# One wait fewer on ScalarE: the exponential of a score tile's first half and VectorE's copy of the second

## The chip, the cores and the metric

The kernel runs on one core of one Trainium2 chip. The metric is device time in microseconds (us) of one launch, the median of several runs. Five engines work side by side, each through its own list of instructions in order: TensorE (PE in the profile, with its weight loads shown apart as PEld), VectorE (DVE), ScalarE (ACT), GpSimd (POOL) and SyncE (SP, which starts the DMA transfers here). An instruction that needs another engine's result waits on a semaphore, and everything behind it on its own engine waits too. Matmul results land in PSUM, which has eight banks; a bank holds 512 float32 values for each of 128 partitions.

## What is computed

The reference mixes an attention branch and a feed-forward branch over the same input `x` (2048 rows of 512):

```python
g = _sigmoid((x * gate_w).sum(-1, keepdims=True))
q = (x @ wq) in 32 heads of 16;  k = x @ wk;  v = x @ wv      # one k and v for all heads
p = _softmax(einsum("bhqd,bkd->bhqk", q, k) * 16 ** -0.5)
a = (p @ v, heads side by side) @ wo
b = (_silu(x @ w_gate) * (x @ w_up)) @ w_down                 # 1792 hidden features
return g * a + (1 - g) * b
```

Everything is float32. The 32 x 2048 x 2048 exponentials of the attention are the bulk of ScalarE's work, and the feed-forward matmuls are run in three terms each (high and low parts), which is the bulk of TensorE's.

## The kernel before

A first stage (to about 48 us) transposes `x` and makes keys, values and the first queries. A second one (to about 141 us) runs the first 16 loop turns of the attention in a simple pattern. The main stage, from 141 us to 1480 us, is made of blocks, and the change is in it. A tail (83 us) multiplies by `wo` and stores the output.

**A block.** The attention is cut into units `u`: one head and 128 keys against all 2048 queries. A block issues the scores of four units, works on their exponentials, and ends with `mix` (L662 to L671), the product of exponentials and values, for four units whose scores are a little older. Each unit has two score tiles, so a block has eight, numbered 0 to 7 here. A score tile `ps` (named `pss` in the profile) is 128 x 1024: two matmuls at L651, one for each half, and each half fills a PSUM bank of its own. Only two score tiles exist (`ps_s` has two buffers), so the matmuls of tile i+2 wait until tile i has been read.

**TensorE's order in a block** is written out in `STEPS = "SSFFFFSFFSFFSFFFSFFFSFFS"`. S is a score tile. F is a step of the feed-forward work: two matmuls side by side in the two halves of the array (L174). So between tile 2 and tile 3 there are two F, and so on. After the last S comes `mix` (L670).

**Who reads a score tile.** `KINDS = "HHHAHHAA"` says it. An A tile (3, 6, 7) is read by ScalarE alone, in one exponential over 1024 columns. An H tile (0, 1, 2, 4, 5) is shared: VectorE copies its second half out of PSUM into the tile `pt` in SBUF (L656), and ScalarE takes the exponential of its first half straight from PSUM (L660, `pt<-pss 128x512`). The second half's exponential is done later, in place in SBUF (L660, `pt<-pt 128x512`).

**ScalarE's order** is the list `EXPS = ("0d", "1d", "0s", "2d", "3d", "4d", "1s", "5d", "6d", "7d", "2s", "4s", "5s")`: `d` is the exponential out of PSUM, `s` the one in place of the copied half. At the end of some blocks a tanh of the feed-forward work follows (L268 or L272).

**VectorE's order** follows the program text: the copies stand behind their score tiles, the evacuations of finished feed-forward tiles in between, and at the end of a block up to 3.6 us (`BUDGET`) of put-off work: the silu product that needs the tanh (L276), splits into high and low parts, reciprocals of the softmax sums (L679).

The framework below the kernel puts in all the semaphore waits. It keeps any two instructions that touch the same tile `ps` in order, so before the change the exponential of an H tile's first half waits for the copy of its second half, though the two touch neither the same PSUM bank nor the same columns of `pt`.

Of the kernel before, what the change touches and what calls it, by code (L numbers as in the profile page):

```python
# [12 lines left out]
AF = mybir.ActivationFunctionType  # L13
# [8 lines left out]
H = 32  # L22
# [4 lines left out]
CH = 512  # L27
# [7 lines left out]
SCALE = DH ** -0.5  # L35
# [26 lines left out]
def tile_gated_mix(ctx, tc, x, wq, wk, wv, wo, w_gate, w_up, w_down, gate_w, out):  # L62
    nc = tc.nc
# [59 lines left out]
    def run(queue, n):  # L123
        for _ in range(min(n, len(queue))):
            queue.pop(0)()
# [502 lines left out]
    with tc.tile_pool(name="bpool", bufs=2) as bp:  # L628
# [11 lines left out]
        def new_pt(u):  # L640
            late = u > PTB * (BEGIN * 2 // PTB) and (u - 2 * BEGIN) % (2 * PTB) >= PTB
            PT[u] = (PAIR[1] if late else bp).tile([P, S], F32, name="pt", bufs=PTB)

        def score(u, j, half=False):
            h, kt = divmod(u, NT)
            if j == 0:
                new_pt(u)
            ps = ps_s.tile([P, 2 * CH], F32, name="pss")
            for b in range(2):
                rows = slice(b * RT, (b + 1) * RT)  # L650
                nc.tensor.matmul(ps[:, b * CH:(b + 1) * CH], ks[rows, kt * P:(kt + 1) * P], QS[h][rows, j, :],  # L651
                                 start=True, stop=True)
            halves.clock += 1
            pt = PT[u][:, j * 2 * CH:(j + 1) * 2 * CH]
            if half:
                nc.vector.tensor_copy(pt[:, CH:], ps[:, CH:])  # L656
            return pt, ps

        def exps(pt, ps, w=slice(None)):
            nc.scalar.activation(pt[:, w], ps[:, w], AF.Exp, scale=SCALE)  # L660

        def mix(u):  # L662
            h, kt = divmod(u, NT)
            pt = PT.pop(u)
            if kt == 0:
                run(COPY, 1)
                PO[:] = [ps_o.tile([P, CH], F32, name="po")]
            po = PO[0]
            for c in range(NCH):
                nc.tensor.matmul(po[c * 2 * DH:(c + 1) * 2 * DH, :], vaug[:, kt, :], pt[:, c * CH:(c + 1) * CH],  # L670
                                 start=(kt == 0), stop=(kt == NT - 1))  # L671
            if kt == NT - 1:

                osb = hp.tile([P, CH], F32, name="osb")
                rsb = hp.tile([P, CH], F32, name="rsb", bufs=1)

                def invert(i):
                    w = slice(i * P, (i + 1) * P)
                    nc.vector.reciprocal(rsb[:, w], rsb[:, w])  # L679

                def store():
                    nc.vector.tensor_tensor(osb, osb, rsb, ALU.mult)
                    for c in range(NCH):
                        nc.sync.dma_start(o_d[h * DH:(h + 1) * DH, c * CH:(c + 1) * CH],
                                          osb[c * 2 * DH:c * 2 * DH + DH, :])

                COPY.append(lambda: nc.vector.tensor_copy(osb, po))
                LATER.extend([(0.6, lambda: nc.vector.stream_shuffle(rsb, osb, [DH] * 2 * DH))] +
                             [(1.0, lambda i=i: invert(i)) for i in range(TC)] + [(0.7, store)])
# [5 lines left out]
        def feed(k, more=True):  # L695
            for _ in range(k):
                if JOBS and more or halves.busy():
                    halves.step(more)

        def block(k, first, last, steps, kinds, order):  # L700
            more = k < NB - STOP
            tiles = [(u, j) for u in range(first, last) for j in range(2)]
            order = list(order)
            made = []

            def emit():
                while order and int(order[0][0]) < len(made):
                    i, how = int(order[0][0]), order.pop(0)[1]
                    pt, ps = made[i]
                    if how == "s":  # L710
                        exps(pt, pt, slice(CH, None))
                    else:
                        exps(pt, ps, slice(0, CH) if kinds[i] == "H" else slice(None))

            for i, what in enumerate(steps):
                if what == "F":
                    feed(1, more)
                elif len(made) < len(tiles):
                    made.append(score(*tiles[len(made)], kinds[len(made)] == "H"))
                    emit()  # L720
                if len(made) > 1:
                    run(COPY, 1)
            due = [e for e in order if int(e[0]) < 2 * (BLOCK * (k + 1) - first)]
            for e in due:
                order.remove(e)
            rest, order[:] = order[:], due
            emit()
            run(ACTS, len(ACTS))
            order[:] = rest
            emit()  # L730
            assert not order and len(made) == len(tiles)
            left = BUDGET
            for queue in (LATER[:1], DEFER, LATER):
                while queue and queue[0][0] <= left:
                    cost, f = queue.pop(0)
                    left -= cost
                    f()
                if queue is not DEFER and queue is not LATER and left < BUDGET:
                    LATER.pop(0)
            for u in range(BLOCK * k, BLOCK * (k + 1)):  # L740
                mix(u)
            halves.clock += 2 * LONG
# [7 lines left out]
        with tc.manual_schedule():  # L750
            for j in range(2):
                exps(*score(0, j))
            for n in range(BEGIN):
                quota = RATE
                u = 2 * n
                if n == 0:
                    feed(FIRST)
                exps(*score(u + 1, 0))
                if n == 0:
                    feed(quota - FIRST)  # L760
                exps(*score(u + 1, 1))
                feed(FIRST)
                exps(*score(u + 2, 0))
                feed(quota - FIRST)
                exps(*score(u + 2, 1))
                settle()
                mix(u)
                mix(u + 1)
                halves.clock += LONG
                run(COPY, 1)  # L770
                if LATER:
                    LATER.pop(0)[1]()
                if n == NT // 2 + 1:
                    load_head(2)
# [59 lines left out]
    with tc.If(rv != 0):  # L834
        with tc.tile_pool(name="gpool", bufs=2) as gp:
            with tc.For_i(0, H, 1) as h:
# [3 lines left out]
                for qt in range(NT):  # L840
# [3 lines left out]
                    for half in range(2):  # L844
                        ps = ps_s.tile([P, 2 * CH], F32, name="pss")
# [8 lines left out]
                    for half in range(2):  # L854
                        nc.scalar.activation(pr[:, half * 2 * CH:(half + 1) * 2 * CH], halves[half], AF.Exp,
                                             scale=SCALE, bias=mx[:, 2:3])
                    po = ps_o.tile([P, CH], F32, name="po")
                    for b in range(NT // TC):
                        pt = ps_f.tile([P, CH], F32, name="pf")
# [48 lines left out]
```

## Time and profile before

| what | value |
|---|---|
| median of 3 runs | 1564.16 us (1563.3 to 1565.58) |
| the profiled execution: its own time | 1565.49 us |
| its span, first to last instruction | 1563.7 us |
| TensorE busy | 1433.5 us (92%) |
| TensorE weight loads | 761.6 us (49%) |
| ScalarE busy | 1089.2 us (70%) |
| VectorE busy | 862.9 us (55%) |
| GpSimd busy | 389.0 us (25%) |
| mean granted TensorE clock | 0.989 |

Busy time of TensorE counts matmuls that overlap, and a matmul that was held up shows a longer duration, so 92% doesn't mean that only 8% could be gained. In a row of the timeline stand the start, the duration, the engine, the source line, the operation, the tiles written and read, the shape and the count; the bracket behind it gives idle time of the engine just before and the instruction that ended it. In the list of waits stand the waiting group, the releasing group, the total in us, how often, and the longest. A group's row gives its busy time and the mean duration in ns.

### The profile page before, as it was taken

The numbers are of one execution on the slowest core, as the hardware profiler recorded it, in microseconds if no ns is written. First come the engines' busy times: TensorE is split into PE (matmuls) and PEld (weight loads), VectorE is DVE, ScalarE is ACT, GpSimd is POOL, SyncE is SP. The second block draws the span as 40 slices with busy tenths as digits, with TensorE's granted clock in tenths as the row PEclk, the third lists the DMA queues.
The fourth block names the chain that finished last, engine by engine and source line by source line (L and its number), as shares of the span: only waits on it lengthen the run. The fifth ranks groups of instructions, "written<-read, shape, count | busy, mean of one in ns | idle before, by whom it ended". The sixth has DMA issues, their size and how long they took to land. (4 is left out here: it accounts for less than half of the span.)

```text
span 1563.7 us, 26910 instructions
## 1 busy us (share of the span) xinstructions
PE 1433.5 (92%) x10755; PEld 761.6 (49%) x10755; DVE 862.9 (55%) x1458; ACT 1089.2 (70%) x1699; POOL 389.0 (25%) x408
## 2 busy tenths in 40 slices
PE   9999999998989988999898988989999889899998
PEld 7654444444444444444444444444444444454476
DVE  5464555565555565556456566456556556465442
ACT  4677777777777767777777777777777777777700
POOL 5041220420220410230130331141131230143153
PEclk9999999999999999999999999999999999999999
DMA  7554211211131310211131221120221120221044
GB/s 244 179 167 119 63 38 31 68 32 41 50 103 31 105 41 24 56 48 36 53 112 31 72 51 45 31 82 25 58 58 30 62 64 25 58 65 51 12 151 143
DMA packets 101493, 107.79 MB, mean 69 GB/s; under 512 B 9969, under 2 KB 69617, under 8 KB 99697
## 3 DMA queue, kind: packets, MB, share of 16 engines
q1 hardware_dynamic: 99632, 105.81, 23.4%
q8 instruction: 86, 1.41, 0.4%
q10 hardware_dynamic: 1728, 0.20, 0.1%
q14 instruction: 47, 0.38, 0.1%
HBM read 76.09 MB, written 29.36 MB: 67 GB/s over the span
## 5 line engine op out<-in xcount | busy, mean ns | idle before, releaser
L660 ACT ACTIVATE pt<-pss 128x512 f32<-128x512 f32 (+1 forms) x1024 | 746.1, 779 | 371.6 <-DVE pt L656 337.5
L656 DVE COPY pt<-pss 128x512 f32<-128x512 f32 x590 | 395.3, 687 | 363.1 <-PE pss L651 356.5
L651 PE MATMUL pss<-qs,ks 64*128 64x512 f32 x2048 | 454.9, 457 | 117.6 <-ACT pt L660 113.4
L670 PE MATMUL po<-pt,vaug 128*32 128x512 f32 x4096 | 467.7, 596 | 0.0
L651 PEld LDWEIGHTS pss<-qs,ks 64*128 64x128 f32 x2048 | 185.5, 186 | 442.1 <-ACT pt L660 329.4
L660 ACT ACTIVATE pt<-pt 128x512 f32<-128x512 f32 x590 | 345.8, 637 | 0.0
L670 PEld LDWEIGHTS po<-pt,vaug 128*32 128x32 f32 x4096 | 119.5, 110 | 258.1 <-issue 257.8
L105 POOL CAST wuh<-wraw 128x512 fp32r<-128x512 f32 x56 | 34.5, 617 | 553.6 <-PE pf L174 431.1
L174 PE MATMUL pf<-xh,wuh 64*128 64x512 f32 (+1 forms) x440 | 168.1, 398 | 0.0
L174 PE MATMUL pf<-xh,wgh 64*128 64x512 f32 (+1 forms) x444 | 167.0, 395 | 0.0
L174 PE MATMUL pf<-xh,wgl 64*128 64x512 f32 (+1 forms) x444 | 166.6, 395 | 0.0
L174 PE MATMUL pf<-xl,wgh 64*128 64x512 f32 (+1 forms) x444 | 166.3, 395 | 0.0
L174 PE MATMUL pf<-xh,wul 64*128 64x512 f32 (+1 forms) x440 | 165.6, 396 | 0.0
L174 PE MATMUL pf<-xl,wuh 64*128 64x512 f32 (+1 forms) x440 | 164.7, 397 | 0.0
L174 PE MATMUL pf<-wdl,hh 64*128 64x512 f32 (+1 forms) x427 | 160.3, 397 | 2.5 <-POOL wdl L106 2.5
L174 PE MATMUL pf<-wdh,hl 64*128 64x512 f32 (+1 forms) x427 | 160.0, 397 | 0.0
L174 PE MATMUL pf<-wdh,hh 64*128 64x512 f32 (+1 forms) x427 | 158.5, 397 | 0.4 <-POOL wdh L105 0.4
L105 POOL CAST wgh<-wraw 128x512 fp32r<-128x512 f32 x56 | 35.2, 629 | 413.7 <-PE pf L174 330.7
L679 DVE RECIPROCAL rsb<-rsb 128x128 f32<-128x128 f32 x128 | 115.9, 931 | 2.8 <-issue 1.2
L276 DVE SCALAR_TENSOR_TENSOR ht<-ht,hs 128x512 f32<-128x512 f32 x48 | 34.1, 711 | 133.2 <-ACT ht L268 133.2
L174 PEld LDWEIGHTS pf<-xl,wuh 64*128 64x128 f32 (+1 forms) x440 | 83.4, 190 | 7.7
L174 PEld LDWEIGHTS pf<-xh,wuh 64*128 64x128 f32 (+1 forms) x440 | 83.5, 190 | 7.0
(157 smaller groups left out, 1637.0 us busy)
## 6 DMA issues: line engine op xcount, KB each, us to landing
wraw<-in_B_w_gate_dram SPq DMA_DIRECT2D x56, 256.0 KB
wraw<-in_B_w_up_dram SPq DMA_DIRECT2D x56, 256.0 KB
wraw<-in_B_w_down_dram SPq DMA_DIRECT2D x56, 256.0 KB
qs<-q_d SPq DMA_DIRECT2D x62, 192.0 KB
q_d<-hl SPq DMA_DIRECT2D x18, 256.0 KB
q_d<-hh SPq DMA_DIRECT2D x18, 256.0 KB
o_d<-osb SPq DMA_DIRECT2D x128, 32.0 KB
a_d<-acc SPq DMA_DIRECT2D x4, 1024.0 KB
```

The source lines that it names most:

```text
L105: eng_hi.tensor_copy(hi, src)
L174: ins = nc.tensor.matmul(self.ps, a, b, start=(i == 0 and not half), stop=(last and half != 0))
L276: nc.vector.scalar_tensor_tensor(t[0], t[0], 1.0, g, op0=ALU.add, op1=ALU.mult)
L651: nc.tensor.matmul(ps[:, b * CH:(b + 1) * CH], ks[rows, kt * P:(kt + 1) * P], QS[h][rows, j, :], start=True, stop=True)
L656: nc.vector.tensor_copy(pt[:, CH:], ps[:, CH:])
L660: nc.scalar.activation(pt[:, w], ps[:, w], AF.Exp, scale=SCALE)
L670: nc.tensor.matmul(po[c * 2 * DH:(c + 1) * 2 * DH, :], vaug[:, kt, :], pt[:, c * CH:(c + 1) * CH], start=(kt == 0), stop=(kt == NT - 1))
L679: nc.vector.reciprocal(rsb[:, w], rsb[:, w])
```

## The change

The function `score` now returns VectorE's copy instruction along with the tile. The function `exps` tells the framework that the exponential of an H tile's first half doesn't depend on that copy. Which instruction stands where on each engine stays the same; what changes is what some of them wait for.

```diff
-            if half:
-                nc.vector.tensor_copy(pt[:, CH:], ps[:, CH:])
-            return pt, ps
-
-        def exps(pt, ps, w=slice(None)):
-            nc.scalar.activation(pt[:, w], ps[:, w], AF.Exp, scale=SCALE)
+            other = nc.vector.tensor_copy(pt[:, CH:], ps[:, CH:]) if half else None
+            return pt, ps, other
+
+        def exps(pt, ps, other=None, w=slice(None)):
+            ins = nc.scalar.activation(pt[:, w], ps[:, w], AF.Exp, scale=SCALE)
+            if other is not None:
+                tc.declare_no_dep(getattr(ins, "ins", ins), getattr(other, "ins", other), reason="another bank")
...
-                    pt, ps = made[i]
+                    pt, ps, other = made[i]
                     if how == "s":
-                        exps(pt, pt, slice(CH, None))
+                        exps(pt, pt, w=slice(CH, None))
                     else:
-                        exps(pt, ps, slice(0, CH) if kinds[i] == "H" else slice(None))
+                        exps(pt, ps, other, slice(0, CH) if kinds[i] == "H" else slice(None))
```

ScalarE, one block of before, its thirteen exponentials in the order of `EXPS`; a name like DVE_49 is the semaphore that counts VectorE's instructions, PE_49 and Activation_49 those of TensorE and ScalarE:

```order
L660 ACTIVATE pt<-pss 128x512 [waits DVE_49,Activation_49]
L660 ACTIVATE pt<-pss 128x512 [waits DVE_49]
L660 ACTIVATE pt<-pt 128x512
L660 ACTIVATE pt<-pss 128x512 [waits DVE_49]
L660 ACTIVATE pt<-pss 128x1024 [waits PE_49]
L660 ACTIVATE pt<-pss 128x512 [waits DVE_49]
L660 ACTIVATE pt<-pt 128x512
L660 ACTIVATE pt<-pss 128x512 [waits DVE_49]
L660 ACTIVATE pt<-pss 128x1024 [waits PE_49,Activation_49]
L660 ACTIVATE pt<-pss 128x1024 [waits PE_49]
L660 ACTIVATE pt<-pt 128x512 x3
```

The same block of the changed kernel (L659 is the same statement, which stands one line higher there):

```order
L659 ACTIVATE pt<-pss 128x512 [waits PE_49,Activation_49]
L659 ACTIVATE pt<-pss 128x512 [waits PE_49]
L659 ACTIVATE pt<-pt 128x512 [waits DVE_49]
L659 ACTIVATE pt<-pss 128x512 [waits PE_49]
L659 ACTIVATE pt<-pss 128x1024 [waits PE_49]
L659 ACTIVATE pt<-pss 128x512 [waits PE_49]
L659 ACTIVATE pt<-pt 128x512 [waits DVE_49]
L659 ACTIVATE pt<-pss 128x512 [waits PE_49]
L659 ACTIVATE pt<-pss 128x1024 [waits PE_49,Activation_49]
L659 ACTIVATE pt<-pss 128x1024 [waits PE_49]
L659 ACTIVATE pt<-pt 128x512 [waits DVE_49] x3
```

Nothing moved. The five exponentials of first halves wait for the score matmul instead of the copy, and the five in place now name the copy, which they had behind them already before.

TensorE, score tiles 2 and 3 of a block, before:

```order
L651 MATMUL pss<-qs,ks 128x512 [waits Activation_49]
L651 MATMUL pss<-qs,ks 128x512
L174 MATMUL pf<-wdh,hl 128x512
L174 MATMUL pf<-wdh,hh 128x512 x2
L174 MATMUL pf<-wdl,hh 128x512
L651 MATMUL pss<-qs,ks 128x512 [waits Activation_49]
```

And in the changed kernel:

```order
L651 MATMUL pss<-qs,ks 128x512 [waits DVE_49,Activation_49]
L651 MATMUL pss<-qs,ks 128x512
L174 MATMUL pf<-wdh,hl 128x512
L174 MATMUL pf<-wdh,hh 128x512 x2
L174 MATMUL pf<-wdl,hh 128x512
L651 MATMUL pss<-qs,ks 128x512 [waits DVE_49,Activation_49]
```

A score tile that reuses the place of an H tile now waits for both of its readers by name. An instruction carries one wait; a second one becomes an instruction of its own ahead of it, EVENT_SEMAPHORE in the profile. So TensorE's list grows by 590 of these, five for each of 118 blocks, and ScalarE's by 28.

## The prediction

> **What bounds the kernel now.** I began with the page's busy times and the list of waits.
>
> ```profile
> PE 1433.5 (92%) x10755; PEld 761.6 (49%) x10755; DVE 862.9 (55%) x1458; ACT 1089.2 (70%) x1699; POOL 389.0 (25%) x408
> ```
>
> ```profile
> ACT pt L660 <- DVE pt L656: 337.5, 344, 4.0
> PEld pss L651 <- ACT pt L660: 329.4, 573, 2.3
> PE pss L651 <- ACT pt L660: 113.4, 240, 1.9
> ```
>
> No engine is full apart from TensorE's 92%, which counts overlapped and held-up matmuls. The three waits form one chain: ScalarE stands 337.5 us behind VectorE's copies, and TensorE's score tiles stand behind ScalarE. The edit cuts the first link. What that is worth depends on when the copy ends compared with the exponential, so I read one ordinary block in the timeline, first TensorE:
>
> ```profile
> 730.84 0.73 PE L651 MATMUL pss<-qs,ks 64*128 64x512 f32 x4
> 731.41 0.39 PE L174 MATMUL pf<-wdl,hh 64*128 64x512 f32 x1
> ...
> 732.10 0.39 PE L174 MATMUL pf<-wdl,hh 64*128 64x512 f32 x1
> ...
> 732.82 0.50 PE L651 MATMUL pss<-qs,ks 64*128 64x512 f32 x2 [0.32 <-ACT pt L660]
> ...
> 733.62 0.40 PE L651 MATMUL pss<-qs,ks 64*128 64x512 f32 x2
> ...
> 734.73 0.50 PE L651 MATMUL pss<-qs,ks 64*128 64x512 f32 x2 [0.25 <-ACT pt L660]
> ...
> 735.77 0.41 PE L651 MATMUL pss<-qs,ks 64*128 64x512 f32 x2
> ...
> 736.73 0.51 PE L651 MATMUL pss<-qs,ks 64*128 64x512 f32 x2
> ...
> 737.73 0.50 PE L651 MATMUL pss<-qs,ks 64*128 64x512 f32 x2
> 738.16 3.64 PE L670 MATMUL po<-pt,vaug 128*32 128x512 f32 x32
> 741.73 0.73 PE L651 MATMUL pss<-qs,ks 64*128 64x512 f32 x4
> ```
>
> Tiles 0 and 1 start at 730.84 and about 731.18, four F steps follow, and the block ends at 741.73: 10.89 us. An undisturbed step takes 0.23 (731.41 to 732.10 is three steps) to 0.24 (735.77 to 736.73 is four); I use 0.235. Against that, tile 2 should start at 731.41 + 4 x 0.235 = 732.35 and starts at 732.82; tile 4 should start three steps after tile 3, at 734.32, and starts at 734.73; tile 7 comes at 737.73 instead of 737.43. A tile that was held also makes the next step 0.1 longer (732.82 to 733.62 is 0.80, not 0.70). Then ScalarE and VectorE in the same stretch:
>
> ```profile
> 732.17 1.13 ACT L660 ACTIVATE pt<-pss 128x512 f32<-128x512 f32 x2 [2.01 <-DVE pt L656]
> 733.20 0.62 ACT L660 ACTIVATE pt<-pt 128x512 f32<-128x512 f32 x1
> 734.09 1.51 ACT L660 ACTIVATE pt<-pss 128x512 f32<-128x512 f32 x2 [0.27 <-DVE sign L394]
> 736.08 0.60 ACT L660 ACTIVATE pt<-pss 128x512 f32<-128x512 f32 x1 [0.48 <-DVE pt L656]
> 736.57 0.62 ACT L660 ACTIVATE pt<-pt 128x512 f32<-128x512 f32 x1
> 737.09 2.42 ACT L660 ACTIVATE pt<-pss 128x512 f32<-128x512 f32 x3
> 739.38 1.69 ACT L660 ACTIVATE pt<-pt 128x512 f32<-128x512 f32 x3
> ```
>
> ```profile
> 731.38 1.29 DVE L656 COPY pt<-pss 128x512 f32<-128x512 f32 x2 [0.74 <-PE pss L651]
> 733.36 0.69 DVE L656 COPY pt<-pss 128x512 f32<-128x512 f32 x1 [0.69 <-PE pss L651]
> ...
> 735.35 0.69 DVE L656 COPY pt<-pss 128x512 f32<-128x512 f32 x1 [1.30 <-PE pss L651]
> 736.22 0.69 DVE L656 COPY pt<-pss 128x512 f32<-128x512 f32 x1 [0.18 <-PE pss L651]
> ```
>
> Each held tile is the same relay. Tile 0's matmul starts at 730.84, the copy runs 731.38 to 732.07, ScalarE starts only at 732.17 (idle for 2.01 before) and ends at 732.77, and TensorE starts tile 2 at 732.82. Copy and exponential stand one behind the other, and the ring of two score tiles passes both on to TensorE.
>
> **The change, an ordinary block replayed by hand.** The wait for the copy goes; the exponential may start when the matmul is done, as the copy does: 0.54 after a tile's start behind `mix` (731.38 - 730.84), 0.44 else (a matmul of 0.40 and a gap of about 0.04). ScalarE starts its 512-column pieces 0.52 apart (736.57 to 737.09) and the 1024-column ones 0.9 apart (737.09 to 739.38 is one short and two long).
>
> - Tile 0: exponential 731.38 to 731.98, copy to 732.07. Tile 1: exponential 731.9 to 732.5, copy to 732.67 (731.38 + 1.29). The in-place piece 0s runs 732.4 to 733.0, its copy long done.
> - Tile 2 needs tile 0 free at 732.07 and is due at 732.35: no wait. Tile 3 is due at 733.05 and needs 732.67.
> - Tile 2's copy runs 732.8 to 733.5, its exponential 732.9 to 733.5, behind 0s. Tile 4 is due at 733.76: no wait.
> - Tile 3 (ScalarE alone) 733.5 to 734.5; tile 5 is due at 734.70. Tile 4's exponential ends at 735.0, its copy at 734.9; tile 6 is due at 735.64. Tile 5's exponential, behind 1s, ends at 736.0 and its copy at 735.8; tile 7 is due at 736.35.
> - Tile 7 to `mix` takes 0.43 as now, `mix` to the next block 3.57 as now: `mix` at 736.78, the next block at 740.35.
>
> So this block takes 9.51 us, not 10.89: 1.38 less. What is late next there is nothing on ScalarE (the smallest margin is about 0.2, ahead of tile 5) but TensorE's own list. ScalarE's 13 pieces take 10 x 0.52 + 3 x 0.9 = 7.9 of the 9.5 us. The new waits of the five in-place pieces cost nothing while the copy is done first, as here; if VectorE were late, everything behind 0s on ScalarE would wait with it, tile 2's exponential first.
>
> How many blocks there are, and how long the mean one is:
>
> ```profile
> L656 DVE COPY pt<-pss x590: 625/691/695, 141.5 to 1472.2; 128x512 f32<-128x512 f32 x197
> ```
>
> 590 copies at five a block are 118 blocks. From the first block's first copy to the last block's last one are 1330.7 us; less the 4.84 between those two in a block (731.38 to 736.22), 1325.9 / 117 = 11.33 us for the mean block, 0.44 over the ordinary one. One of those that are longer:
>
> ```profile
> 706.59 0.69 DVE L276 SCALAR_TENSOR_TENSOR ht<-ht,hs 128x512 f32<-128x512 f32 x1 [3.82 <-ACT ht L268]
> ...
> 707.97 0.39 PE L174 MATMUL pf<-wdl,hh 64*128 64x512 f32 x1
> ...
> 708.17 0.69 DVE L682 TENSOR_TENSOR osb<-osb,rsb 128x512 f32<-128x512 f32 x1
> ...
> 708.78 1.28 DVE L656 COPY pt<-pss 128x512 f32<-128x512 f32 x2
> ...
> 709.56 1.14 ACT L660 ACTIVATE pt<-pss 128x512 f32<-128x512 f32 x2 [3.01 <-DVE pt L656]
> ...
> 710.21 0.56 PE L651 MATMUL pss<-qs,ks 64*128 64x512 f32 x2 [1.85 <-ACT pt L660]
> ```
>
> Here VectorE sat behind the tanh, then worked off what was put off, and copied tile 0 only at 708.78. Tile 2 was due at 707.97 + 0.235 = 708.2 and came at 710.21, 2.0 late. After the edit it still needs the copy, done at 709.45, so it comes at 709.5, 1.3 late: it saves 0.7 at this tile where the ordinary block saves 0.47. The excess of long blocks therefore does not grow; I carry the 0.44 over whole.
>
> The sum: 9.51 + 0.44 = 9.95 us. I add 0.05 for VectorE, which has less room once blocks are shorter: 10.0, 1.33 less than 11.33. Times 118: 157 us. The profiled execution took 1565.5 (span 1563.7), so 1408.5; the median of the runs lies 1.3 below it: 1407.
>
> ```profile
> 48.00:141.00 93.00, 92.05 (x730) 48.51 (x730) 48.67 (x86) 72.45 (x77) 21.69 (x23) 1.00 0.57 185
> 141.00:1480.00 1339.00, 1222.54 (x9434) 619.67 (x9434) 758.52 (x1282) 994.88 (x1589) 302.81 (x314) 0.99 0.19 51
> ...
> 703.13:716.44 13.31, 11.43 (x82) 6.45 (x80) 6.58 (x11) 8.85 (x15) 2.43 (x3) 0.87 0.36 88
> ```
>
> (Stretch, its length, busy PE, PEld, DVE, ACT, POOL, then granted clock, DMA share, GB/s.) VectorE's 758.5 us over 118 blocks are 6.4 of 10.0, ScalarE's 994.9 are 8.4, and DMA is at 0.19: feeding weights 13% faster has room. Stages outside 141 to 1480 have no H tile and stay.
>
> **Clock.** The long block had a clock of 0.87 after its 1.85 us stall: 13.31 x 0.13 = 1.7 us lost. Over the stage the loss is 0.01 x 1339 = 13 us; shorter stalls may save up to that, which I leave to the range's low end. The Trainium skill ("TensorE: Matmul & The Clock Gate", on why this matters) drops the clock after idle gaps over about 3 us; by it no stall here would have dropped it, and the sum would stay without the 13 us. The trace differs: the half clock followed a gap of 1.85.
>
> **The price of the double waits.**
>
> ```profile
> L651 PEldq EVENT_SEMAPHORE  x71: 51/51/51, 43.8 to 1437.4; - x71
> ```
>
> TensorE gets 590 more such instructions. Between nothing, if they pass while the 0.39 us matmul ahead runs, and 590 x 0.051 = 30 us, if each lies on the path. I take nothing, since a weight load of 0.19 hides in the same place, and keep 1437 for the range. The Trainium skill ("Perfetto Trace Analysis", identifying dependency chains) says that an instruction waiting on several engines may have such instructions put before it; that speaks against this change, and no time is given there.
>
> **The rivals.**
>
> - *VectorE becomes the bound.* Copies then decide tiles 2, 4 and 7 in most blocks. For: the margins are 0.2 to 0.3. Against: VectorE has 3.6 us free per block. If each of those three tiles came 0.17 late, a block would take 10.5: 0.83 x 118 = 98 us saved, 1467.
> - *The two readers of one tile slow each other*, so that copy and exponential take as long together as in turn: no change, about 1564. Against: the exponential at 736.08 and the copy at 736.22 ran together on two tiles in the usual 0.60 and 0.69.
> - *Slower: the extra instruction ahead of a score tile breaks TensorE's weight prefetch.* Each of 590 tiles would pay 0.051 and the 0.1 that a held tile shows: 89 us. It decides only if it exceeds the 157 saved, so if the readers of a tile also slow each other: 1653 with no gain left. Against: it needs both.
>
> **The numbers.** Executions of this kernel lie up to 0.15% apart (1563.3 to 1565.58), so a change within 0.2% can't be told from none. My forecast, 1378 to 1437, has 0.72; VectorE as the bound, 1437 to 1500, 0.18; no change 0.04; slower 0.06. The low end is 1407 less 13 for the clock and less 16 if long blocks lose 0.14 of their excess; the high end 1470 takes in most of the second case. Faster 0.90, same 0.04, slower 0.06.
>
> **What would show it.** In the profile after, ScalarE's wait for the copies should shrink from 337.5 us to under 100, with the rest in front of in-place pieces; TensorE's 113.4 should shrink to some 40 and name VectorE; an ordinary block should take 9.5 us with tiles 2, 4 and 7 on the beat, and a first half's exponential still 0.60 us. Longer exponentials or copies would mean contention; ordinary blocks over 10 us would make the prediction wrong.

## The result and the profile after

The changed kernel takes 1412.79 us (median of 4 runs, 1408.9 to 1414.72), the kernel before 1564.87 (4 runs). The ratio is 0.902, with a 95% interval of 0.900 to 0.905. The profiled execution took 1414.56 us with a span of 1412.8. Two executions at a lower granted clock, 1622.99 us of the kernel before (0.849) and 1885.12 us of the kernel with only tiles 0 and 1 freed (0.654), are left out of all ratios and medians.

The page of the changed kernel, its busy times:

```profile
PE 1351.1 (96%) x10755; PEld 812.5 (58%) x10755; DVE 860.7 (61%) x1458; ACT 1090.5 (77%) x1699; POOL 389.8 (28%) x408
```

ScalarE and VectorE do the work they did before (1089.2 and 862.9 us then) in a shorter span. TensorE's busy time fell by 82 us from 1433.5. A score matmul that isn't held up shows a shorter duration (422 ns in the mean, 457 before), but the score matmuls' own row fell only from 454.9 to 438.4 us; where the rest lies is not shown.

Rows of the list of waits:

```profile
ACT pt L659 <- PE pss L651: 165.0, 210, 3.2
...
DVE ht L276 <- ACT ht L268: 118.9, 48, 4.3
...
PEld pss L651 <- ACT pt L659: 82.1, 184, 1.4
...
PE pss L651 <- DVE pt L655: 36.8, 43, 2.2
...
ACT pt L659 <- DVE pt L655: 30.5, 32, 2.1
```

ScalarE's wait for copies fell from 337.5 to 30.5 us; it now waits for score matmuls. The wait of TensorE's weight loads for ScalarE fell from 329.4 to 82.1. TensorE's own wait at score tiles, 113.4 us for ScalarE before, is 36.8 us for VectorE and 2.8 for ScalarE. An ordinary block in the timeline, where VectorE has no late work, TensorE's rows (the feed-forward steps are left out):

```profile
562.23 3.64 PE L671 MATMUL po<-pt,vaug 128*32 128x512 f32 x32
565.80 0.73 PE L651 MATMUL pss<-qs,ks 64*128 64x512 f32 x4
567.29 0.49 PE L651 MATMUL pss<-qs,ks 64*128 64x512 f32 x2
568.05 0.42 PE L651 MATMUL pss<-qs,ks 64*128 64x512 f32 x2
568.73 0.47 PE L651 MATMUL pss<-qs,ks 64*128 64x512 f32 x2
569.66 0.46 PE L651 MATMUL pss<-qs,ks 64*128 64x512 f32 x2
570.62 0.43 PE L651 MATMUL pss<-qs,ks 64*128 64x512 f32 x2
571.32 0.44 PE L651 MATMUL pss<-qs,ks 64*128 64x512 f32 x2
571.69 3.64 PE L671 MATMUL po<-pt,vaug 128*32 128x512 f32 x32
```

and ScalarE and VectorE at its start:

```profile
566.40 1.08 ACT L659 ACTIVATE pt<-pss 128x512 f32<-128x512 f32 x2 [1.38 <-PE pss L651]
```

```profile
566.44 1.29 DVE L655 COPY pt<-pss 128x512 f32<-128x512 f32 x2 [4.79 <-PE pss L651]
```

From `mix` to `mix` the block takes 9.46 us. Exponential and copy of tile 0 start together, at 566.40 and 566.44, and tile 2 follows 1.49 after tile 0 where it took 1.98. No row of TensorE in this block has a bracket: nothing is held.

A long block of the changed kernel, VectorE and then TensorE:

```profile
1104.29 0.69 DVE L276 SCALAR_TENSOR_TENSOR ht<-ht,hs 128x512 f32<-128x512 f32 x1 [2.27 <-ACT ht L268]
1104.90 1.76 DVE L680 RECIPROCAL rsb<-rsb 128x128 f32<-128x128 f32 x2
1106.58 1.22 DVE L655 COPY pt<-pss 128x512 f32<-128x512 f32 x2
```

```profile
1104.36 0.73 PE L651 MATMUL pss<-qs,ks 64*128 64x512 f32 x4
1107.35 0.50 PE L651 MATMUL pss<-qs,ks 64*128 64x512 f32 x2 [1.33 <-DVE pt L655]
```

Here VectorE waits for the tanh, works off two reciprocals and copies tile 0 only at 1106.58, so tile 2 is held for 1.33 us, now by VectorE itself. And a block of a third kind, VectorE:

```profile
585.73 1.29 DVE L655 COPY pt<-pss 128x512 f32<-128x512 f32 x2 [1.77 <-PE pss L651]
586.94 0.68 DVE L259 COPY hs<-pf 128x512 f32<-128x512 f32 x1
587.54 0.68 DVE L655 COPY pt<-pss 128x512 f32<-128x512 f32 x1
```

and TensorE's tiles 3 and 4:

```profile
587.35 0.41 PE L651 MATMUL pss<-qs,ks 64*128 64x512 f32 x2
588.37 0.50 PE L651 MATMUL pss<-qs,ks 64*128 64x512 f32 x2
```

An evacuation (L259) stands ahead of tile 2's copy, which ends at 588.22; tile 4 starts at 588.37, 1.02 after tile 3 where the block above has 0.68.

The timelines hold every block, so the blocks can be counted. Of 117 blocks 37 take 9.55 us or less; the median block takes 9.83, the mean one 10.05. So the block shown first is one of the shortest third. The mean stretches between the starts of score tiles, over the blocks whose rows are all there (117 of 118 before, 116 after), in us, with what the prediction forecast for an ordinary block:

| from tile to tile | before | after | saved | forecast |
|---|---|---|---|---|
| 0 to 2 | 2.31 | 1.85 | 0.47 | 0.47 |
| 2 to 3 | 0.82 | 0.74 | 0.07 | 0.10 |
| 3 to 4 | 1.15 | 0.90 | 0.25 | 0.41 |
| 4 to 5 | 1.08 | 0.98 | 0.11 | 0.10 |
| 5 to 6 | 0.96 | 0.95 | 0.02 | 0 |
| 6 to 7 | 1.00 | 0.70 | 0.30 | 0.30 |
| 7 to the next 0 | 4.00 | 3.94 | 0.06 | 0 |

Tiles 2, 5 and 7 gave what was forecast, tile 3 a little less, and tile 4 much less. In 36 of the 116 blocks tile 2 comes over 1.6 us behind tile 0 (1.49 on its beat), as in the long block. In 57 tile 4 comes over 0.8 us behind tile 3 (0.68 in the block shown first). In 50 of these VectorE evacuates something between the copies of tiles 1 and 2, as in the block of the third kind, and no block with such an evacuation has tile 4 on its beat.

### The profile page after: what moved, and what is told of

It reads as the page before. It is cut to its first block, busy times and chain, and to the rows that moved or that the text cites. A ratio compares the mean times of both kernels' runs of the same rounds, so it can differ in the third digit from the quotient of the medians.

```text
span 1412.8 us, 27527 instructions
## 1 busy us (share of the span) xinstructions
PE 1351.1 (96%) x10755; PEld 812.5 (58%) x10755; DVE 860.7 (61%) x1458; ACT 1090.5 (77%) x1699; POOL 389.8 (28%) x408
## 5 line engine op out<-in xcount | busy, mean ns | idle before, releaser
L659 ACT ACTIVATE pt<-pss 128x512 f32<-128x512 f32 (+1 forms) x1024 | 756.0, 778 | 187.6 <-PE pss L651 165.0
L651 PE MATMUL pss<-qs,ks 64*128 64x512 f32 x2048 | 438.4, 422 | 49.1 <-DVE pt L655 36.8
L659 ACT ACTIVATE pt<-pt 128x512 f32<-128x512 f32 x590 | 345.6, 630 | 30.8 <-DVE pt L655 30.5
L651 PEld LDWEIGHTS pss<-qs,ks 64*128 64x128 f32 x2048 | 206.4, 184 | 251.1 <-issue 142.4
L174 PE MATMUL pf<-xh,wuh 64*128 64x512 f32 (+1 forms) x440 | 164.1, 391 | 0.0
L174 PE MATMUL pf<-xh,wul 64*128 64x512 f32 (+1 forms) x440 | 162.0, 390 | 0.0
L174 PE MATMUL pf<-xl,wuh 64*128 64x512 f32 (+1 forms) x440 | 160.3, 390 | 0.0
L174 PE MATMUL pf<-wdh,hl 64*128 64x512 f32 (+1 forms) x427 | 156.8, 392 | 0.0
L174 PE MATMUL pf<-wdh,hh 64*128 64x512 f32 (+1 forms) x427 | 155.5, 392 | 0.4 <-POOL wdh L105 0.4
L276 DVE SCALAR_TENSOR_TENSOR ht<-ht,hs 128x512 f32<-128x512 f32 x48 | 36.9, 770 | 118.9 <-ACT ht L268 118.9
L174 PEld LDWEIGHTS pf<-xh,wgh 64*128 64x128 f32 (+1 forms) x444 | 82.5, 186 | 4.9
L174 PEld LDWEIGHTS pf<-xh,wgl 64*128 64x128 f32 (+1 forms) x444 | 82.7, 187 | 4.4
```

Source lines behind the costliest of these rows:

```text
L174: ins = nc.tensor.matmul(self.ps, a, b, start=(i == 0 and not half), stop=(last and half != 0))
L276: nc.vector.scalar_tensor_tensor(t[0], t[0], 1.0, g, op0=ALU.add, op1=ALU.mult)
L659: ins = nc.scalar.activation(pt[:, w], ps[:, w], AF.Exp, scale=SCALE)
```

## The experiments

Each kernel was timed in several rounds beside the kernel before. The theory: copy and exponential of one tile stand one behind the other like a relay, and this holds single score tiles on TensorE. The first rival: ScalarE as a whole runs ahead, and each wait cut gives its share.

**Only tiles 1 and 4 freed.**

```diff
-                        exps(pt, ps, other, slice(0, CH) if kinds[i] == "H" else slice(None))
+                        exps(pt, ps, other if i in (1, 4) else None, slice(0, CH) if kinds[i] == "H" else slice(None))
```

> The changed kernel, but only the exponentials of tiles 1 and 4 are freed from the copy; 0, 2 and 5 wait as before. Theory (a relay of copy and exponential that holds single tiles): tiles 3 and 6, which reuse the places of 1 and 4, were not held before, so little comes of it, about 0.1 us a block through an earlier tile 5: 10 to 20 us saved, about 1550 us. Rival (every wait cut gives its share, since ScalarE as a whole is ahead): two of five waits, about 61 of the 152 us saved, about 1504 us.

Measured: 1556.56 us, ratio 0.995 (0.993 to 0.996), 9 us saved, just under the relay's 10 to 20 and far from the shares' 61. Two of the five waits are gone and next to nothing comes of it, so the shares theory falls. Waits of this run:

```profile
ACT pt L659 <- DVE pt L655: 331.8, 323, 4.0
PEld pss L651 <- ACT pt L659: 305.4, 475, 2.4
```

ScalarE waits for VectorE almost as long as before: it takes its exponentials in order, and the one it stands in front of is still tied to its copy.

**Only tiles 0 and 1 freed.** The same line with `(0, 1)`.

> Only tiles 0 and 1 freed. Theory (relay): tile 2 comes on its beat (0.47 and the 0.1 of a held tile), tiles 4 and 7 stay held: 0.57 us a block, 67 us saved, about 1498 us. Rival (shares): the same two of five as in the run with tiles 1 and 4, so the same time as that run.

Measured: 1517.30 us, ratio 0.971 (0.968 to 0.974), by which 46 us of the 152 are saved. The same number of waits as in the run before gives five times as much, as the relay says, but less than its 67. One block, TensorE:

```profile
601.48 0.73 PE L651 MATMUL pss<-qs,ks 64*128 64x512 f32 x4
602.96 0.50 PE L651 MATMUL pss<-qs,ks 64*128 64x512 f32 x2
603.72 0.43 PE L651 MATMUL pss<-qs,ks 64*128 64x512 f32 x2
604.87 0.56 PE L651 MATMUL pss<-qs,ks 64*128 64x512 f32 x2 [0.26 <-ACT pt L659]
605.90 0.46 PE L651 MATMUL pss<-qs,ks 64*128 64x512 f32 x2
606.91 0.50 PE L651 MATMUL pss<-qs,ks 64*128 64x512 f32 x2
607.92 0.49 PE L651 MATMUL pss<-qs,ks 64*128 64x512 f32 x2
608.34 3.64 PE L671 MATMUL po<-pt,vaug 128*32 128x512 f32 x32
611.91 0.51 PE L651 MATMUL pss<-qs,ks 64*128 64x512 f32 x2
```

Tile 2 is on its beat (1.48 after tile 0), and tile 4 comes 1.15 after tile 3, late by 0.45 where it was late by 0.41. The block takes 10.43 us, 0.46 less than 10.89. So I counted too much by adding the 0.1 of a held tile: tile 3 still comes 0.76 after tile 2. The rest of the shortfall lies at tile 4 in other blocks. Over all 118 blocks the stretch from tile 3 to tile 4 takes 1.39 us in the mean, where it took 1.15 before: 1.65 in the 46 blocks with an evacuation ahead of tile 2's copy (1.19 before) and 1.21 in the other 72 (1.12 before). So most of it goes with that evacuation; that the tied exponential passes it on to TensorE fits these numbers, and was not tried by itself.

**Tiles 0, 1 and 2 freed.** The same line with `(0, 1, 2)`.

> Tiles 0, 1 and 2 freed, 4 and 5 wait for their copies. Theory (relay): tiles 2 and 4 on the beat, tile 7 about 0.3 us late and the next step 0.1 longer: 1.0 us a block saved, about 118 us, so 1447 us. Rival (shares): three of five, 91 us, 1474 us.

Measured: 1462.69 us, ratio 0.935 (0.933 to 0.938), 102 us saved: 16 us more time than the relay's 1447 and 11 less than the shares' 1474. By itself it leans to neither, but the ladder does: 46 us with tiles 0 and 1, 56 more with tile 2, 50 more with tiles 4 and 5, and 9 for tiles 1 and 4 when 0, 2 and 5 are tied. (An estimated 14 us of the first step came with a higher granted clock; see the clock below.)

**The price of the double waits.** In the kernel before, a memset behind each copy, and the score matmul made to wait for it as well; beside it the same kernel without the second wait.

```diff
+        READ = []
...
-                nc.tensor.matmul(ps[:, b * CH:(b + 1) * CH], ks[rows, kt * P:(kt + 1) * P], QS[h][rows, j, :],
+                ins = nc.tensor.matmul(ps[:, b * CH:(b + 1) * CH], ks[rows, kt * P:(kt + 1) * P], QS[h][rows, j, :],
...
+                if b == 0 and len(READ) > 1 and READ[-2] is not None:
+                    follow(ins, READ[-2])
+            READ.append(None)
...
                 nc.vector.tensor_copy(pt[:, CH:], ps[:, CH:])
+                READ[-1] = nc.vector.memset(sign, 0.0)
```

> The kernel before with nothing freed, but with the 590 double waits: a 0.06 us memset follows each copy on VectorE, and the matmul that reuses the tile's place waits for it as well as for ScalarE. The memset is over long before the exponential, so the second wait is always met already. Theory (a met second wait hides under the matmul ahead): the same time as the run with the memsets alone, within 4 us. Rival (an extra instruction of 0.051 us ahead of each of 590 tiles lies on the path, with or without the loss of the weight prefetch): 30 to 89 us more than that run.

> The kernel before with the memset behind each copy but without the second wait on TensorE: what the memsets cost by themselves. Both theories: 590 x 0.06 = 35 us of VectorE's time that lies mostly in its idle stretches, 0 to 15 us more than the kernel before.

Measured, in five rounds: 1566.04 us with the second wait and 1566.05 without, ratios to the kernel before 1.0008 (0.9996 to 1.0021) and 1.0009 (0.9998 to 1.0020). The rows of the score tiles' extra instructions, with and then without the second wait (count, then shortest, median and longest in ns):

```profile
L653 PEldq EVENT_SEMAPHORE  x661: 51/51/697, 44.1 to 1472.6; - x166
```

```profile
L653 PEldq EVENT_SEMAPHORE  x71: 51/51/51, 44.7 to 1440.3; - x71
```

590 more of them, and no time. By itself this doesn't exclude a price, for in this kernel TensorE still stands 438.9 us behind ScalarE at the score tiles, and a delay of 0.05 us could vanish in such a wait. The changed kernel's own beat leaves little room for one. In the block at 565.80 tiles 2 to 7 start at 567.29 to 571.32, 4.03 us, where 17 steps of 0.235 ask for 4.00; the four second waits between them, at tiles 3, 4, 6 and 7, would add 0.20 at 0.051 each. The rival of 30 to 89 us falls.

**What is left: the tanh earlier.** All five waits cut, and ScalarE takes the tanh ahead of the last three in-place exponentials.

```diff
             order = list(order)
+            late = order[-3:] if order[-1] == "5s" else []
+            order = order[:len(order) - len(late)]
...
             run(ACTS, len(ACTS))
-            order[:] = rest
+            order[:] = rest + late
             emit()
```

> The changed kernel with all five waits cut, and besides ScalarE takes the tanh of the feed-forward work ahead of the block's last three in-place exponentials (2s, 4s, 5s) instead of behind them, some 1.6 us earlier. Theory (what is left over the ordinary block comes from VectorE's first copy, late behind the product that waits for the tanh, 0.34 us a block in the mean): most of it goes, 25 to 45 us, 1370 to 1390 us. Rival (VectorE is late because of its own work, not the wait): under 10 us, 1403 us or more.

Measured: 1371.17 us, ratio 0.877 (0.875 to 0.879), 42 us less than the changed kernel. VectorE and TensorE in a block with a tanh:

```profile
603.52 0.63 ACT L268 ACTIVATE ht<-hs 128x512 f32<-128x512 f32 x1
604.03 1.67 ACT L659 ACTIVATE pt<-pt 128x512 f32<-128x512 f32 x3
...
604.81 0.68 DVE L276 SCALAR_TENSOR_TENSOR ht<-ht,hs 128x512 f32<-128x512 f32 x1
605.79 0.73 PE L651 MATMUL pss<-qs,ks 64*128 64x512 f32 x4
606.36 1.29 DVE L655 COPY pt<-pss 128x512 f32<-128x512 f32 x2 [0.86 <-PE pss L651]
...
607.29 0.41 PE L651 MATMUL pss<-qs,ks 64*128 64x512 f32 x2
```

VectorE is idle for 0.86 us ahead of the copies and tile 2 is on its beat: the lateness was the wait, not VectorE's own work. Over all blocks tile 2 comes 1.51 us after tile 0 in the mean, where it came after 1.85: 0.34 x 118 = 40 us. In the list of waits the product's wait fell from 118.9 us to this:

```profile
DVE ht L276 <- ACT ht L268: 56.8, 38, 2.8
```

**And tile 2's copy first.** Besides, what VectorE evacuates between the copies of tiles 1 and 2 is put behind tile 2's copy.

```diff
-                self.end(self.ps)
...
+                def done():
+                    self.end(self.ps)
...
+                if half is None or not HOLD[0]:
+                    done()
+                else:
+                    ENDS.append(done)
...
+                HOLD[0] = len(made) == 2 and kinds[2] == "H"
                 if what == "F":
                     feed(1, more)
...
+                if what != "F":
+                    run(ENDS, len(ENDS))
-                if len(made) > 1:
+                if len(made) > 2 or len(tiles) < 3 or kinds[2] != "H" and len(made) > 1:
                     run(COPY, 1)
```

> The kernel with all five waits cut and the tanh early, and besides VectorE's evacuation of a feed-forward tile (or of the attention output) that falls between the copies of tiles 1 and 2 is put behind tile 2's copy. Theory (what still holds tile 4 by 0.19 us in the mean is that evacuation, 0.68 us long, ahead of the copy): 0.21 us a block, about 25 us, 1342 to 1352 us. Rival (tile 4 is then held by ScalarE's own order, or the late evacuation holds a feed-forward tile): under 8 us, 1363 us or more.

Measured: 1354.38 us, ratio 0.865 (0.864 to 0.866), 17 us less than with the tanh alone: the theory holds, at two thirds of its size. Over all blocks the stretch from tile 3 to tile 4 fell from 0.90 to 0.70 us, 0.2 x 118 = 24 us, and no block has tile 4 late any more. The stretch from tile 4 to tile 5 grew by 0.04, 5 us, since in 26 blocks tile 5 is now over 0.1 us late; what holds it there was not followed up. It is the fastest kernel here. Its page, and its score matmuls in the groups of instructions:

```profile
PE 1334.4 (99%) x10755; PEld 807.0 (60%) x10755; DVE 870.3 (64%) x1458; ACT 1079.5 (80%) x1699; POOL 390.9 (29%) x408
```

```profile
L658 PE MATMUL pss<-qs,ks 64*128 64x512 f32 x2048 | 428.4, 416 | 3.2 <-DVE pt L662 1.9 <-ACT pt L666 1.1
```

TensorE's idle time at score tiles is down to 3.2 us. What bounds the main stage now is mainly TensorE's own list.

## Why the prediction was right

- **The relay.** As predicted: cut, the ordinary block takes 9.46 us (9.51 forecast), with tiles 2, 4 and 7 on the beat. The ladder of partial edits and the table of stretches show that the gain sits where tiles were held.
- **Nothing else late in an ordinary block.** Right for the block replayed, whose margins of about 0.2 us held, and for about a third of the blocks. I replayed a block without an evacuation ahead of tile 2's copy; with one, tile 4 is late, and that takes 0.16 of the 0.41 us forecast there.
- **The excess of long blocks.** Carried over at 0.44 and 0.05 added for VectorE, 0.49 in all; the mean block is (1321.7 - 142.3 - 3.7) / 117 = 10.05, so the excess was 0.59. The two numbers are the first and last copy's start in this row, and 3.7 is the stretch between a block's first and last copy (566.44 to 570.16):

```profile
L655 DVE COPY pt<-pss x590: 623/691/694, 142.3 to 1321.7; 128x512 f32<-128x512 f32 x197
```

  The term that was too small is VectorE's 0.05: once tile 4 isn't held by the relay, an evacuation ahead of tile 2's copy holds it. Putting that copy first, in the kernel with the early tanh, gave 17 us, 0.14 a block. The ordinary block came out 0.05 under its forecast and the excess 0.10 over it; the difference, 0.05 x 118, is the 6 us between 1407 and 1412.8. That it is so little is in part luck: 0.08 us a block of what was saved stands at tiles 5 to 6 and 7 to 0, where nothing was forecast, and the clock, which the sum left out, is in these means too.
- **The double waits.** Taken at nothing, and at most 0.03 us a block, 4 us in all, is left for those at tiles 3, 4, 6 and 7 in the beat of the changed kernel's ordinary block.
- **Two readers of one tile.** They don't slow each other: first halves' exponentials took 596 ns in the mean before the edit and after it, while copy and exponential now start together on the two banks of a tile. The copies kept their median of 691 ns. The group's row of before, then of after (the second number behind the bar is the mean in ns):

```profile
L660 ACT ACTIVATE pt<-pss 128x512 f32<-128x512 f32 x590 | 346.3, 596 | 345.5 <-DVE pt L656 337.5 <-DVE sign L394 6.8
```

```profile
L659 ACT ACTIVATE pt<-pss 128x512 f32<-128x512 f32 x590 | 339.5, 596 | 127.0 <-PE pss L651 125.0
```

  The Trainium skill ("PSUM — Partial Sum Buffer", on bank collisions) says that two engines on different banks run clean, and that in one bank and the same group of 32 partitions they collide. The first is the condition on which this edit rests, and the trace agrees with it; the second no run here shows.
- **Clock.** The stage's granted clock rose from 0.99 to 1.00 as the stalls shortened, within the 13 us that I had left to the low end. In stretches of 2 us, the profiled execution of before has eight places in this stage where the clock falls, each worth some 1.7 us like the one at 710 us, and that of the changed kernel two; the kernel with tiles 0 and 1 freed has none. So an estimated 10 of the 152 us (6 x 1.7) came with the clock and not from the relay's length. Only how stalls and clock changed together is seen; how long a stall drops the clock was not tried. Before, all eight drops lie in blocks whose tile 2 came about 3.5 us or more after tile 0, where 1.98 is the median; seven other blocks of that kind show no drop. The stage after, with the clock third from the end:

```profile
141.00:1330.00 1189.00, 1140.90 (x9446) 669.79 (x9442) 757.17 (x1283) 997.28 (x1591) 305.00 (x315) 1.00 0.21 58
```

## What to carry to other kernels

When two engines share a buffer and neither needs the other's part, look at what the framework makes of it: a dependency by tile can put them one behind the other, and in a ring of two buffers that sum is paid by the engine that fills it. Price such a wait by replaying one block from the timeline, tile by tile, and not by its total: two of the five waits were worth 9 us or 46, depending on which tiles they stood at. Then count in how many blocks the replay holds; here an evacuation broke it at one tile in 50 of 116. When it is gone, look at once for what stands ahead of the slower reader; moving two pieces of work out of its way brought another 58 us.

## What the hardware showed

A second wait on a matmul costs nothing measurable when it is already met. 590 more EVENT_SEMAPHORE instructions of 51 ns changed the time by 0.01 us, with intervals of about 0.12% (2 us), in a kernel whose TensorE also waits otherwise. In the changed kernel's ordinary block, where it doesn't, five tiles with four such waits among them take 4.03 us against 4.00 at the beat. I had kept up to 30 us for them.
